# Operands moved to multiples of 512 bytes, and 768 tokens taken as 512 + 256 moving columns

## Chip, cores and metric

One core of a Trainium2 chip. The metric is the device time of one execution in microseconds, the median of the runs shown. The kernel is written in Bass with Tile: instructions go to TensorE, VectorE, ScalarE and GpSimd (PE, DVE, ACT and POOL below), DMAs are issued from SyncE's queue (SP). Outside the attention part the order on each engine is laid by the compiler's scheduler, starting from the program's order.

## What is computed

Two sequences (batch 2) of 768 tokens pass three layers, all in float32:

- block attention, 8 heads of width 64: each query sees the keys less than 16 positions away, and one summary (the largest of 32 keys, the mean of 32 values) for each block of 32 tokens; the result is x, 768 x 512;
- a gated layer: h = relu(x w_in), split into u and v (512 each); v is normalised over its 512 features and mixed over the tokens, v_s = w_spatial v_n + b; the result is (u * v_s) w_out;
- a convolution layer: h = relu(x w_in2) (1024 features), a depthwise convolution over the tokens with three taps, then (h * sigmoid(conv)) w_out2.

```
v_s = einsum('ts,bsd->btd', w_spatial, v_n) + b_spatial[None, :, None]
x   = (u * v_s) @ w_out
h   = relu(x @ w_in2);  c[t] = w0 * h[t-1] + w1 * h[t] + w2 * h[t+1]
out = (h * sigmoid(c)) @ w_out2
```

## The kernel before, in words

**Matmuls.** All large products are of float32 accuracy: each operand is held as a high part (rounded to float32r) and a low part (what is left), side by side in one tile of [128, 2, n], and `mm3` (line 58) issues three matmuls for each 128 x 128 stationary block: high x high (L62), high x low (L63), low x high (L64). The stationary operand is `lhsT`, 128 columns; the moving one, `rhs`, has as many columns as the output. `split` (line 66) makes high and low parts: a copy on ScalarE (L70), a subtraction on GpSimd or VectorE (L73).

**Stages**, in order:

- Attention, lines 179 to 325: 24 groups of 256 queries (8 pairs of heads and batch, 3 groups each), ordered by hand: `Plan` (line 133) lays a list by costs and due times, and the instructions are issued in this order. Idle TensorE time takes pieces of f1u for batch 0 (`f1u_plan`, line 413): one piece for each pair c, with its cost, with rank 1000 (after everything else that is ready), reading the token groups of x that its columns need. Six of the eight token halves go here.
- f1v(b), line 389: v = relu(x w_in) for a tile of 128 tokens; stationary x, moving w1, 512 columns (tile vps). Then statistics, normalising, high and low part of vn (L367 to L385).
- f1u(b), line 402: u = relu(x w_in) with features on the partitions; stationary w1, moving x, twice 384 tokens (ups; mm for the pieces in the attention part).
- spatial(b), line 429: stationary vn, moving wsp (the mixing matrix), twice 384 tokens, 6 blocks x 3 matmuls each (sps); then bias, product with u, high and low part of g1.
- merge_weights, line 457: w_out w_in2 as one matrix; stationary wo, moving wi, 512 columns (wps), result in wp.
- i2(b), line 476: eight tiles f of 128 features; stationary wp, moving g1, twice 384 tokens (hps), 4 blocks x 3 matmuls each. A relu on ScalarE writes h into hh, which has a zero column on either side (two memsets on VectorE, L480 and L481). The first tap is a scaled copy on ScalarE (L487), the two others are a multiply and add on VectorE (L489); then sigmoid (L490), product on GpSimd (L491), high and low part of y (low part on GpSimd in batch 0, on VectorE in batch 1).
- o2(b), line 505: stationary y, moving w2, 512 columns (ops); for three token tiles the feature tiles 0 to 6 first, then feature tile 7; the last token tile of batch 1 in two halves of 256 columns. A copy and a DMA out.

The order after attention (lines 606 to 620): f1v(0), f1u(0) (the rest), spatial(0), f1v(1), f1u(1), spatial(1), merge_weights, i2(0), o2(0), i2(1), o2(1), with the weights' loading and conversion beside them.

**Places in SBUF.** Tiles come from pools that lie one behind the other: const, slots (X tiles for x and g1, V tiles for u, vn and wp, W tiles for w1, wi and w2), tmp, then, when the attention pool is closed, late on its memory: b_bc, S tiles (wsp, then y 0 to 5), T tiles (wst, wo, hh and ct), raw and last, Y tiles (y 6 and 7). A tile's size is rounded up to 32 bytes in a partition. In tmp there are five tiles of 2048 bytes and ten small ones of 32.

Of the kernel before, what the change touches and what calls it, by code (L numbers as in the profile page):

```python
# [32 lines left out]
DM = 512  # L33
DF = 1024
NT = S // 128
HS = S // 2


@with_exitstack
def block_kernel(ctx, tc, q_in, k_in, vwin, v_in, mask, runs, w_in, w_spT, b_sp, w_outT, w_in2, conv, w_out2, out):  # L40
# [3 lines left out]
    const = ctx.enter_context(tc.tile_pool(name="const", bufs=1))  # L44
    slots = ctx.enter_context(tc.tile_pool(name="slots", bufs=1))
    tmp = ctx.enter_context(tc.tile_pool(name="tmp", bufs=5))
    psm = ctx.enter_context(tc.tile_pool(name="psm", bufs=2, space=PSUM))

    mm_pools = [psm, None, 0]
# [8 lines left out]
    def mm3(ps, pairs, first=True, last=True):  # L58

        n = len(pairs)  # L60
        for i, ((lh, ll), (rh, rl)) in enumerate(pairs):
            PE.matmul(ps, lhsT=lh, rhs=rh, start=first and i == 0, stop=False)  # L62
            PE.matmul(ps, lhsT=lh, rhs=rl, start=False, stop=False)  # L63
            PE.matmul(ps, lhsT=ll, rhs=rh, start=False, stop=last and i == n - 1)  # L64
# [328 lines left out]
            yield  # L393

    def f1u_mm(ps, b, f, h, c):
        fs, hs = slice(f * 128, (f + 1) * 128), slice(h * HS, (h + 1) * HS)
        mm3(ps[:, :HS], [((w1[c, 0][:, 0, fs], w1[c, 0][:, 1, fs]), (x[b, c][:, 0, hs], x[b, c][:, 1, hs]))], first=c == 0, last=c == NP - 1)

    def f1u_relu(ps, b, f, h):
        ACT.activation(out=u[b, f // 2][:, f % 2, h * HS:(h + 1) * HS], in_=ps[:, :HS], func=AF.Relu)  # L400

    def f1u(b, first=0):
        if not first:
# [9 lines left out]
    def f1u_plan(k, bank):  # L413

        f, h = divmod(k, 2)
        ps, m = mms[bank], ("mm", bank)
        for c in range(NP):
            xs = [("x", 0, c, g) + e for g in ((0, 1), (1, 2))[h] for e in ((), ("h",))]
            plan.add({"PE": (0.53, lambda c=c: f1u_mm(ps, 0, f, h, c))}, 1000 + k, xs + [("w1h", c, 0), ("w1l", c, 0)] + [m] * bool(c), [m])
        plan.add({"ACT": (0.49, lambda: f1u_relu(ps, 0, f, h))}, STEP * 12 + k, [m], [("u", k)])  # L420

    def load_wsp():
        for t in range(NT):
            wsp.append(late.tile([128, 2, S], F32R, tag="S", name=f"wsp_{t}", bufs=6))
            st = t_slot(f"wst_{t}", F32)[:, 0, :S]
            SP.dma_start(st, w_spT[t * 128:(t + 1) * 128, :])
            split(st, wsp[t][:, 0], wsp[t][:, 1], leng=POOL if t % 2 else DVE)

    def spatial(b):
        for f in range(4):  # L430
            g1[b, f] = x_slot(f"g_{b}_{f}")
            for h in range(2):
                ps = mmps(f"sps_{b}_{f}_{h}")
                fs, hs = slice(f * 128, (f + 1) * 128), slice(h * HS, (h + 1) * HS)
                mm3(ps[:, :HS], [((vn[b][2 * t][:, fs], vn[b][2 * t + 1][:, fs]), (wsp[t][:, 0, hs], wsp[t][:, 1, hs])) for t in range(NT)])
                tt = tmp.tile([128, HS], F32, tag="tmp", name=f"tt_{b}_{f}_{h}")
                DVE.tensor_tensor(out=tt, in0=ps[:, :HS], in1=b_bc[:, hs], op=ALU.add)
                DVE.tensor_tensor(out=tt, in0=tt, in1=u[b, f // 2][:, f % 2, hs], op=ALU.mult)
                split(tt, g1[b, f][:, 0, hs], g1[b, f][:, 1, hs], heng=ACT, leng=DVE)
                yield  # L440
# [35 lines left out]
    def i2(b):  # L476
        for f in range(8):
            tt = t_slot(f"hh_{b}_{f}", F32)
            hh, ct = tt[:, 0], tt[:, 1, :S]
            DVE.memset(hh[:, 0:1], 0.0)  # L480
            DVE.memset(hh[:, S + 1:S + 2], 0.0)  # L481
            for h in range(2):
                ps = mmps(f"hps_{b}_{f}_{h}")
                fs, hs = slice(f % 4 * 128, (f % 4 + 1) * 128), slice(h * HS, (h + 1) * HS)
                mm3(ps[:, :HS], [((wp(c, f // 4)[0][:, fs], wp(c, f // 4)[1][:, fs]), (g1[b, c][:, 0, hs], g1[b, c][:, 1, hs])) for c in range(4)])
                ACT.activation(out=hh[:, 1 + h * HS:1 + (h + 1) * HS], in_=ps[:, :HS], func=AF.Relu)
            ACT.activation(out=ct, in_=hh[:, 0:S], func=AF.Copy, scale=conv_t[:, 3 * f:3 * f + 1])  # L487
            for j in (1, 2):
                DVE.scalar_tensor_tensor(out=ct, in0=hh[:, j:j + S], scalar=conv_t[:, 3 * f + j:3 * f + j + 1], in1=ct, op0=ALU.mult, op1=ALU.add)  # L489
            ACT.activation(out=ct, in_=ct, func=AF.Sigmoid)  # L490
            POOL.tensor_tensor(out=ct, in0=hh[:, 1:S + 1], in1=ct, op=ALU.mult)  # L491
            if f < 6:
                y[b, f] = late.tile([128, 2, S], F32R, tag="S", name=f"y_{b}_{f}", bufs=6)
            else:
                y[b, f] = late.tile([128, 2, S], F32R, tag="Y", name=f"y_{b}_{f}", bufs=2)
            split(ct, y[b, f][:, 0], y[b, f][:, 1], heng=ACT, leng=DVE if b else POOL)
            yield

# [102 lines left out]
    raw_pool[0] = late  # L601

    def t_slot(name, dt):
        return late.tile([128, 2, S + 2], dt, tag="T", name=name, bufs=3)

    b_bc = late.tile([128, S], F32, name="b_bc", bufs=1)
    SP.dma_start(b_bc, b_sp.partition_broadcast(128))
# [71 lines left out]
```

## Time and profile before

| | |
|---|---|
| median of 3 runs | 360.98 us (360.39 to 361.37) |
| span of the profiled execution | 358.8 us; no other time is listed for it |
| TensorE busy | 345.1 us, 2487 matmuls |
| VectorE, ScalarE, GpSimd busy | 229.4, 183.4, 157.9 us |

The span goes from the first instruction to the last. Matmuls are pipelined: the duration shown of one (0.33 us at 384 columns) reaches into the next, so the pace is read from the distance of starts. A window's row gives its bounds, its length, then for each engine the busy time and the number of instructions that touch the window, and last the granted clock of TensorE, the DMA share and GB/s. A count can hold one or two matmuls that only reach over an edge; where the bounds are the first starts of two neighbouring stages, and only the stage's tile is asked for, it is the stage's own number.

### The profile page before, as it was taken

Reading aid. Unit: us, or ns where it says so; the run is one execution under the profiler, and the core shown is the slowest. Engines: PE = TensorE matmul, PEld = TensorE weight load, DVE = VectorE, ACT = ScalarE, POOL = GpSimd, SP = SyncE. Lnnn points to the kernel's source line nnn. Section 1 sums busy time; section 2 is a strip of 40 time slices with the busy share of each in tenths; the row PEclk is TensorE's granted clock in tenths of the full one; section 3 lists DMA queues with packets and bytes.
Section 4 is the critical chain, followed back from the end, with each engine's and each line's share of the span. In section 5 each row is a group of like instructions: output and inputs, shape, how many; then the busy total and the mean of one; then the engine's idle time right before and its main releaser. Section 6 shows DMA issues by size and latency. Waiting matters only on the chain.

```text
span 358.8 us, 6400 instructions
## 1 busy us (share of the span) xinstructions
PE 345.1 (96%) x2487; PEld 301.0 (84%) x2487; DVE 229.4 (64%) x390; ACT 183.4 (51%) x374; POOL 157.9 (44%) x159
## 2 busy tenths in 40 slices
PE   8998899999797999999999999999999999999996
PEld 4766677777586999899999888999888899998885
DVE  3889998884179799779298899457620025886000
ACT  2766778757264442355342464867531047874101
POOL 3789999765136142116133062587870003333000
PEclk9999999999899899999999999999999999999999
DMA  8877888320381232015232351000002020000202
GB/s 259 276 231 239 235 265 248 98 68 2 94 293 43 58 103 74 0 35 164 97 107 71 108 166 78 2 0 0 2 0 88 2 88 1 3 0 2 88 0 88
DMA packets 11118, 33.86 MB, mean 94 GB/s; under 512 B 1488, under 2 KB 1872, under 8 KB 11088
## 3 DMA queue, kind: packets, MB, share of 16 engines
q1 hardware_dynamic: 11088, 33.46, 29.8%
q8 instruction: 19, 0.31, 0.3%
q14 instruction: 11, 0.09, 0.1%
HBM read 30.31 MB, written 3.15 MB: 93 GB/s over the span
## 4 chain that ended last, share of the span: by engine, by line
PE 86%; DVE 4%; DMA 3%; POOL 2%; issue 2%; ACT 1%; SPq 0%; POOLq 0%; ACTq 0%; DVEq 0%
PE ops L63 6%; PE ops L62 6%; PE ops L64 6%; PE hps L62 6%; PE hps L63 6%; PE hps L64 6%; PE sps L64 5%; PE sps L62 5%; PE sps L63 5%; PE xp L310 3%; PE s L284 3%; PE pt L305 3%; PE mm L247 2%; PE vps L62 2%; PE wps L64 2%; PE wps L63 2%
## 5 line engine op out<-in xcount | busy, mean ns | idle before, releaser
L489 DVE SCALAR_TENSOR_TENSOR hh<-hh,conv_t 128x768 f32<-128x768 f32 x32 | 43.2, 1349 | 41.9 <-ACT hh L487 41.4
L491 POOL TENSOR_TENSOR hh<-hh 128x768 f32<-128x768 f32 x16 | 25.4, 1588 | 53.7 <-ACT hh L490 53.7
L63 PE MATMUL hps<-g,wp 128*128 128x384 f32 x128 | 42.8, 334 | 0.0
L64 PE MATMUL hps<-g,wp 128*128 128x384 f32 x128 | 42.8, 334 | 0.0
L62 PE MATMUL hps<-g,wp 128*128 128x384 f32 x128 | 42.8, 334 | 0.0
L62 PE MATMUL ops<-w,y 128*128 128x512 f32 (+1 forms) x104 | 39.0, 377 | 0.0
L63 PE MATMUL ops<-w,y 128*128 128x512 f32 (+1 forms) x104 | 38.9, 377 | 0.0
L64 PE MATMUL ops<-w,y 128*128 128x512 f32 (+1 forms) x104 | 37.8, 376 | 0.0
L62 PE MATMUL sps<-wsp,vn 128*128 128x384 f32 x96 | 32.9, 343 | 1.8 <-ACT vn L382 1.8
L64 PE MATMUL sps<-wsp,vn 128*128 128x384 f32 x96 | 32.7, 345 | 0.5 <-DVE vn L385 0.5
L63 PE MATMUL sps<-wsp,vn 128*128 128x384 f32 x96 | 32.9, 343 | 0.0
L301 POOL TENSOR_TENSOR e<-e,st 128x480 f32<-128x480 f32 x24 | 25.4, 1061 | 15.6 <-DVE st L298 5.3
L292 ACT ACTIVATE e<-s,st 128x120 f32<-128x120 f32 x96 | 26.8, 371 | 7.2 <-DVE st L288 7.1
L517 ACT COPY o<-ops 128x512 f32<-128x512 f32 (+1 forms) x13 | 6.8, 557 | 40.0 <-PE ops L64 39.5
L62 PEld LDWEIGHTS hps<-g,wp 128*128 128x128 f32 x128 | 24.0, 188 | 0.1
L63 PEld LDWEIGHTS hps<-g,wp 128*128 128x128 f32 x128 | 24.0, 188 | 0.1
L64 PEld LDWEIGHTS hps<-g,wp 128*128 128x128 f32 x128 | 24.0, 188 | 0.0
L64 PEld LDWEIGHTS ops<-w,y 128*128 128x128 f32 x104 | 19.5, 188 | 4.0
L62 PEld LDWEIGHTS ops<-w,y 128*128 128x128 f32 x104 | 19.5, 187 | 4.0
L63 PEld LDWEIGHTS ops<-w,y 128*128 128x128 f32 x104 | 19.5, 188 | 3.9
L73 POOL TENSOR_TENSOR wi<-wit_f,wi 128x512 fp32r<-128x512 f32 x8 | 12.8, 1604 | 20.4 <-ACT wi L70 20.4
L73 POOL TENSOR_TENSOR w<-w2t_f,w 128x512 fp32r<-128x512 f32 x8 | 11.9, 1519 | 20.5 <-ACT w L70 20.5
(121 smaller groups left out, 874.8 us busy)
## 6 DMA issues: line engine op xcount, KB each, us to landing
vw<-vwin SPq DMA_DIRECT2D x8, 576.0 KB, 5.5
raw<-w_in SPq DMA_DIRECT2D x8, 512.0 KB, 4.9
wit_raw<-w_in SPq DMA_DIRECT2D x8, 512.0 KB, 3.7
w2t_raw<-w_out SPq DMA_DIRECT2D x8, 512.0 KB, 3.7
kt<-k_in SPq DMA_DIRECT2D x8, 400.0 KB, 4.6
qt<-q_in SPq DMA_DIRECT2D x8, 384.0 KB, 3.6
out<-o SPq DMA_DIRECT2D x11, 256.0 KB, 2.0
wst<-w_spT SPq DMA_DIRECT2D x6, 384.0 KB, 4.9
```

What stands on the lines that cost most here:

```text
L62: PE.matmul(ps, lhsT=lh, rhs=rh, start=first and i == 0, stop=False)
L63: PE.matmul(ps, lhsT=lh, rhs=rl, start=False, stop=False)
L64: PE.matmul(ps, lhsT=ll, rhs=rh, start=False, stop=last and i == n - 1)
L73: leng.tensor_tensor(out=lo, in0=src, in1=hi.bitcast(F32), op=ALU.subtract)
L247: PE.matmul(ps, lhsT=runs_t[:, NZ - WK - 2 * blk:NZ - WK - 2 * blk + NK], rhs=vws[j][:WK, blk], start=blk == 0, stop=blk == NB - 1)
L284: PE.matmul(s[c * QB:(c + 1) * QB, h, a * NK:(a + 1) * NK], lhsT=qts[j][rows, blk * QB:(blk + 1) * QB], rhs=kws[j][rows, blk], start=False ...
L292: ACT.activation(out=e[:, u, :NK], in_=sv[:, u // 2, u % 2], func=AF.Exp, bias=st[:, 0, u:u + 1])
L301: POOL.tensor_tensor(out=e[:, :, :NK], in0=e[:, :, :NK], in1=st[:, 2].unsqueeze(2).to_broadcast([128, GB, NK]), op=ALU.mult)
L305: PE.transpose(pt[:, u], e[:, u, :NK], ident)
L310: PE.matmul(xp[h * D:(h + 1) * D, k * QB:(k + 1) * QB], lhsT=vws[j][:, g * GB + k, h * D:(h + 1) * D], rhs=pts[:, 2 * h + k // 2, k % 2 * ...
L489: DVE.scalar_tensor_tensor(out=ct, in0=hh[:, j:j + S], scalar=conv_t[:, 3 * f + j:3 * f + j + 1], in1=ct, op0=ALU.mult, op1=ALU.add)
L491: POOL.tensor_tensor(out=ct, in0=hh[:, 1:S + 1], in1=ct, op=ALU.mult)
```

## The change

`tmp` gets one more tile of 48 floats, which nothing uses. The halves of 384 tokens become `TS`, 512 and 256 tokens, in f1u (and its planned pieces, with new costs; the short one reads token group 2 alone), in spatial and in i2. T tiles lose two columns: hh has no zero columns any more, the middle tap is the scaled copy, and the two outer taps are added over 767 columns each. S tiles are eight instead of six, and y 6 and 7 come from them too; the Y tiles go.

```diff
--- before.py
+++ after.py
@@ -33,7 +33,7 @@
 DM = 512
 DF = 1024
 NT = S // 128
-HS = S // 2
+TS = [slice(0, 512), slice(512, S)]
 
 
 @with_exitstack
@@ -44,6 +44,7 @@
     const = ctx.enter_context(tc.tile_pool(name="const", bufs=1))
     slots = ctx.enter_context(tc.tile_pool(name="slots", bufs=1))
     tmp = ctx.enter_context(tc.tile_pool(name="tmp", bufs=5))
+    tmp.tile([128, 48], F32, tag="pad", name="pad", bufs=1)
     psm = ctx.enter_context(tc.tile_pool(name="psm", bufs=2, space=PSUM))
 
     mm_pools = [psm, None, 0]
@@ -393,11 +394,11 @@
             yield
 
     def f1u_mm(ps, b, f, h, c):
-        fs, hs = slice(f * 128, (f + 1) * 128), slice(h * HS, (h + 1) * HS)
-        mm3(ps[:, :HS], [((w1[c, 0][:, 0, fs], w1[c, 0][:, 1, fs]), (x[b, c][:, 0, hs], x[b, c][:, 1, hs]))], first=c == 0, last=c == NP - 1)
+        fs, hs = slice(f * 128, (f + 1) * 128), TS[h]
+        mm3(ps[:, :hs.stop - hs.start], [((w1[c, 0][:, 0, fs], w1[c, 0][:, 1, fs]), (x[b, c][:, 0, hs], x[b, c][:, 1, hs]))], first=c == 0, last=c == NP - 1)
 
     def f1u_relu(ps, b, f, h):
-        ACT.activation(out=u[b, f // 2][:, f % 2, h * HS:(h + 1) * HS], in_=ps[:, :HS], func=AF.Relu)
+        ACT.activation(out=u[b, f // 2][:, f % 2, TS[h]], in_=ps[:, :TS[h].stop - TS[h].start], func=AF.Relu)
 
     def f1u(b, first=0):
         if not first:
@@ -415,13 +416,13 @@
         f, h = divmod(k, 2)
         ps, m = mms[bank], ("mm", bank)
         for c in range(NP):
-            xs = [("x", 0, c, g) + e for g in ((0, 1), (1, 2))[h] for e in ((), ("h",))]
-            plan.add({"PE": (0.53, lambda c=c: f1u_mm(ps, 0, f, h, c))}, 1000 + k, xs + [("w1h", c, 0), ("w1l", c, 0)] + [m] * bool(c), [m])
-        plan.add({"ACT": (0.49, lambda: f1u_relu(ps, 0, f, h))}, STEP * 12 + k, [m], [("u", k)])
+            xs = [("x", 0, c, g) + e for g in ((0, 1), (2,))[h] for e in ((), ("h",))]
+            plan.add({"PE": ((0.69, 0.36)[h], lambda c=c: f1u_mm(ps, 0, f, h, c))}, 1000 + k, xs + [("w1h", c, 0), ("w1l", c, 0)] + [m] * bool(c), [m])
+        plan.add({"ACT": ((0.6, 0.38)[h], lambda: f1u_relu(ps, 0, f, h))}, STEP * 12 + k, [m], [("u", k)])
 
     def load_wsp():
         for t in range(NT):
-            wsp.append(late.tile([128, 2, S], F32R, tag="S", name=f"wsp_{t}", bufs=6))
+            wsp.append(late.tile([128, 2, S], F32R, tag="S", name=f"wsp_{t}", bufs=8))
             st = t_slot(f"wst_{t}", F32)[:, 0, :S]
             SP.dma_start(st, w_spT[t * 128:(t + 1) * 128, :])
             split(st, wsp[t][:, 0], wsp[t][:, 1], leng=POOL if t % 2 else DVE)
@@ -431,10 +432,11 @@
             g1[b, f] = x_slot(f"g_{b}_{f}")
             for h in range(2):
                 ps = mmps(f"sps_{b}_{f}_{h}")
-                fs, hs = slice(f * 128, (f + 1) * 128), slice(h * HS, (h + 1) * HS)
-                mm3(ps[:, :HS], [((vn[b][2 * t][:, fs], vn[b][2 * t + 1][:, fs]), (wsp[t][:, 0, hs], wsp[t][:, 1, hs])) for t in range(NT)])
-                tt = tmp.tile([128, HS], F32, tag="tmp", name=f"tt_{b}_{f}_{h}")
-                DVE.tensor_tensor(out=tt, in0=ps[:, :HS], in1=b_bc[:, hs], op=ALU.add)
+                fs, hs = slice(f * 128, (f + 1) * 128), TS[h]
+                n = hs.stop - hs.start
+                mm3(ps[:, :n], [((vn[b][2 * t][:, fs], vn[b][2 * t + 1][:, fs]), (wsp[t][:, 0, hs], wsp[t][:, 1, hs])) for t in range(NT)])
+                tt = tmp.tile([128, n], F32, tag="tmp", name=f"tt_{b}_{f}_{h}")
+                DVE.tensor_tensor(out=tt, in0=ps[:, :n], in1=b_bc[:, hs], op=ALU.add)
                 DVE.tensor_tensor(out=tt, in0=tt, in1=u[b, f // 2][:, f % 2, hs], op=ALU.mult)
                 split(tt, g1[b, f][:, 0, hs], g1[b, f][:, 1, hs], heng=ACT, leng=DVE)
                 yield
@@ -476,23 +478,19 @@
     def i2(b):
         for f in range(8):
             tt = t_slot(f"hh_{b}_{f}", F32)
-            hh, ct = tt[:, 0], tt[:, 1, :S]
-            DVE.memset(hh[:, 0:1], 0.0)
-            DVE.memset(hh[:, S + 1:S + 2], 0.0)
+            hh, ct = tt[:, 0], tt[:, 1]
             for h in range(2):
                 ps = mmps(f"hps_{b}_{f}_{h}")
-                fs, hs = slice(f % 4 * 128, (f % 4 + 1) * 128), slice(h * HS, (h + 1) * HS)
-                mm3(ps[:, :HS], [((wp(c, f // 4)[0][:, fs], wp(c, f // 4)[1][:, fs]), (g1[b, c][:, 0, hs], g1[b, c][:, 1, hs])) for c in range(4)])
-                ACT.activation(out=hh[:, 1 + h * HS:1 + (h + 1) * HS], in_=ps[:, :HS], func=AF.Relu)
-            ACT.activation(out=ct, in_=hh[:, 0:S], func=AF.Copy, scale=conv_t[:, 3 * f:3 * f + 1])
-            for j in (1, 2):
-                DVE.scalar_tensor_tensor(out=ct, in0=hh[:, j:j + S], scalar=conv_t[:, 3 * f + j:3 * f + j + 1], in1=ct, op0=ALU.mult, op1=ALU.add)
+                fs, hs = slice(f % 4 * 128, (f % 4 + 1) * 128), TS[h]
+                n = hs.stop - hs.start
+                mm3(ps[:, :n], [((wp(c, f // 4)[0][:, fs], wp(c, f // 4)[1][:, fs]), (g1[b, c][:, 0, hs], g1[b, c][:, 1, hs])) for c in range(4)])
+                ACT.activation(out=hh[:, hs], in_=ps[:, :n], func=AF.Relu)
+            ACT.activation(out=ct, in_=hh, func=AF.Copy, scale=conv_t[:, 3 * f + 1:3 * f + 2])
+            for j, to, of in ((0, slice(1, S), slice(0, S - 1)), (2, slice(0, S - 1), slice(1, S))):
+                DVE.scalar_tensor_tensor(out=ct[:, to], in0=hh[:, of], scalar=conv_t[:, 3 * f + j:3 * f + j + 1], in1=ct[:, to], op0=ALU.mult, op1=ALU.add)
             ACT.activation(out=ct, in_=ct, func=AF.Sigmoid)
-            POOL.tensor_tensor(out=ct, in0=hh[:, 1:S + 1], in1=ct, op=ALU.mult)
-            if f < 6:
-                y[b, f] = late.tile([128, 2, S], F32R, tag="S", name=f"y_{b}_{f}", bufs=6)
-            else:
-                y[b, f] = late.tile([128, 2, S], F32R, tag="Y", name=f"y_{b}_{f}", bufs=2)
+            POOL.tensor_tensor(out=ct, in0=hh, in1=ct, op=ALU.mult)
+            y[b, f] = late.tile([128, 2, S], F32R, tag="S", name=f"y_{b}_{f}", bufs=8)
             split(ct, y[b, f][:, 0], y[b, f][:, 1], heng=ACT, leng=DVE if b else POOL)
             yield
 
@@ -601,7 +599,7 @@
     raw_pool[0] = late
 
     def t_slot(name, dt):
-        return late.tile([128, 2, S + 2], dt, tag="T", name=name, bufs=3)
+        return late.tile([128, 2, S], dt, tag="T", name=name, bufs=3)
 
     b_bc = late.tile([128, S], F32, name="b_bc", bufs=1)
     SP.dma_start(b_bc, b_sp.partition_broadcast(128))
```

## Rows read from the trace of the kernel before

**Rows 1.** The page: busy time; busy tenths and granted clock in 40 slices.

```profile
PE 345.1 (96%) x2487; PEld 301.0 (84%) x2487; DVE 229.4 (64%) x390; ACT 183.4 (51%) x374; POOL 157.9 (44%) x159
...
PE   8998899999797999999999999999999999999996
...
PEclk9999999999899899999999999999999999999999
```

**Rows 2.** Windows by stage, one tile each: f1v(1), f1u(1), spatial(1), merge_weights, i2(0), o2(0).

```profile
141.23:157.57 16.34, 16.34 (x72) 13.34 (x72) 2.99 (x5) 1.00 0.00 0
...
157.57:174.23 16.66, 16.66 (x96) 16.50 (x95) 3.41 (x7) 1.00 0.41 128
...
174.23:199.19 24.96, 24.96 (x144) 24.80 (x144) 3.86 (x7) 1.00 0.28 85
...
199.19:221.42 22.23, 22.23 (x96) 17.84 (x96) 4.11 (x6) 3.74 (x7) 1.00 0.46 142
...
221.42:254.71 33.29, 33.29 (x192) 33.12 (x191) 6.85 (x14) 1.00 0.00 1
...
254.71:288.25 33.54, 33.54 (x144) 26.81 (x144) 2.65 (x5) 1.00 0.06 24
```

**Rows 3.** Timeline of TensorE, 256-column matmuls of o2(1): start, duration.

```profile
348.23 0.28 PE L63 MATMUL ops<-w,y 128*128 128x256 f32 x1
...
349.93 0.28 PE L63 MATMUL ops<-w,y 128*128 128x256 f32 x1
...
350.64 0.28 PE L63 MATMUL ops<-w,y 128*128 128x256 f32 x1
...
352.53 0.28 PE L64 MATMUL ops<-w,y 128*128 128x256 f32 x1
```

**Rows 4.** Windows with tile sps alone: spatial(0), its start, the stretch behind it.

```profile
111.89:141.23 29.34, 27.07 (x144) 26.24 (x144) 3.79 (x7) 0.94 0.25 72
111.89:115.90 4.01, 1.82 (x8) 1.15 (x8) 0.00 (x0) 1.00 0.00 0
115.90:119.70 3.80, 3.71 (x12) 3.72 (x13) 0.00 (x0) 0.55 0.00 0
```

**Rows 5.** Window over the end of attention: PE, PEld, DVE, ACT, POOL.

```profile
85.00:95.00 10.00, 7.53 (x78) 5.69 (x76) 3.23 (x8) 5.55 (x16) 4.60 (x6) 1.00 0.01 2
```

**Rows 6.** The convolution's tile hh: count, ns min/median/max, first and last start.

```profile
L486 ACT ACTIVATE hh<-hps x32: 468/492/498, 224.8 to 322.1; 128x384 f32<-128x384 f32 x32
L489 DVE SCALAR_TENSOR_TENSOR hh<-hh,conv_t x32: 1018/1052/2190, 227.3 to 326.6; 128x768 f32<-128x768 f32 x32
L480 DVE MEMSET hh<- x16: 59/59/59, 224.2 to 319.8; 128x1 f32 x16
...
L487 ACT ACTIVATE hh<-hh,conv_t x16: 921/927/942, 226.3 to 324.0; 128x768 f32<-128x768 f32 x16
L490 ACT ACTIVATE hh<-hh x16: 842/848/853, 229.8 to 327.7; 128x768 f32<-128x768 f32 x16
...
L70 ACT CAST y<-hh x16: 817/836/840, 232.4 to 330.2; 128x768 fp32r<-128x768 f32 x16
...
L73 DVE TENSOR_TENSOR y<-hh,y x8: 951/953/959, 300.5 to 331.0; 128x768 fp32r<-128x768 f32 x8
```

**Rows 7.** Timeline of GpSimd at the end of i2(0)'s products and low parts.

```profile
262.35 2.33 POOL L73 TENSOR_TENSOR y<-hh,y 128x768 fp32r<-128x768 f32 x1 [0.95 <-ACT y L70]
264.64 1.54 POOL L491 TENSOR_TENSOR hh<-hh 128x768 f32<-128x768 f32 x1
267.13 1.55 POOL L73 TENSOR_TENSOR y<-hh,y 128x768 fp32r<-128x768 f32 x1 [0.94 <-ACT y L70]
```

**Rows 8.** Timeline of TensorE at the start of spatial(0), with its waits.

```profile
113.37 0.44 PE L64 MATMUL sps<-wsp,vn 128*128 128x384 f32 x1 [0.45 <-DVE vn L385]
...
115.98 0.45 PE L62 MATMUL sps<-wsp,vn 128*128 128x384 f32 x1 [1.82 <-ACT vn L382]
```

## Prediction, made before the result

> **What bounds the kernel now.** I read the page first: TensorE is busy for 96% of the span, in nearly every slice, and its granted clock is full in all but a few [rows 1]. So time can only be won where TensorE's own work gets shorter, or where the few holes are. A busy share says nothing of pace, since the matmuls overlap. So the second view is one window for each stage, cut from the stage's first matmul to the next stage's first: length divided by count is the **spacing**, the distance from one matmul's start to the next [rows 2]. Spacings of that view, and of single rows of the timeline:
>
> - 384 columns: 33.29/192 = 173.4 ns in i2 (batch 0), 173.3 in spatial(1), 173.5 in f1u(1) [rows 2].
> - 512 columns: 16.34/72 = 226.9 in f1v(1), but 22.23/96 = 231.6 in merge_weights and 33.54/144 = 232.9 in o2(0) [rows 2]. Same shape and type, full clock in all three.
> - 256 columns, the last token tile of o2(1): 15 steps from 348.23 to 349.93, 113.4 ns, for the first output half; 16 steps from 350.64 to 352.53, 118.1 ns, for the second [rows 3].
>
> At 2.4 GHz the columns alone take 160.0, 213.3 and 106.7 ns. What is on top is 13.4 at 384, 13.6 at 512 in f1v, 18 to 20 at 512 in merge_weights and o2, and 6.7 or 11.4 at 256. Two things follow. Something other than the shape parts f1v from o2; and a 256 seems cheaper than its share of a 384.
>
> The something is, I think, the place of the stationary operand. The pools lie one behind the other, so a tile's place follows from the sizes before it. The pool `slots` (X, V, W) starts on a multiple of 512 bytes and its tiles are multiples of 512. `tmp` is 5 x 2048 + 10 x 32 = 10,560 bytes, 320 more than a multiple, so the pool `late` starts 320 past one: wsp and y 0 to 5 lie at 320, y 6 and 7 at 416, the T tiles of wo at 320, 352 and 384 (S + 2 makes each a little over 6144). So f1v has both operands on 512; merge_weights has wo off it; o2 has y off it. In spatial(1) only the moving operand (wsp) is off, and its spacing equals that of i2, where nothing is off. So a moving operand off 512 costs nothing visible at 384 columns, and a stationary one costs 5 to 6 ns at 512.
>
> **The change, part by part.**
>
> *Pad and T tiles without the two extra columns.* 48 floats are 192 bytes: 320 + 192 = 512, so wsp, wo and y come onto 512. No instruction is added. o2: 11 whole token tiles x 24 = 264 matmuls x (232.9 - 226.9) = 1.58 us. merge_weights: 96 x (231.6 - 226.9) = 0.45 us. The 48 of 256 columns in o2: the first half already stands at 113.4, so I take 0 (at most 24 x 4.7 ns = 0.11).
>
> *384 + 384 becomes 512 + 256.* The number of matmuls and columns stays. A pair takes 2 x 173.4 = 346.8 ns now. After, both operands are on 512, so the 512 is nearest to f1v's row, 226.9. For the 256 no row has everything aligned: from below 106.7 ns, the columns' time alone, from above 120.3, if it carried 13.6 like its neighbours; I take the measured 113.4. Pair: 340.3, a gain of 6.5 ns; the ends of the 256 make it +13.2 and -0.4, and the slowest rows (232.9 + 118.1 = 351.0) make it a loss of 4.2. Pairs on the path: i2 2 x 192, spatial(1) 144 and f1u(1) 96 matmuls, and what spatial(0) still has to do after its wait (144 less the 8 and 12 of the first 7.8 us, 124) [rows 2, 4], give 192 + 72 + 48 + 62 = 374 pairs. 374 x 6.5 = 2.43 us. The 36 pairs in the attention part and the 12 of f1u(0) before that wait I count at nothing: in 85 to 95 us TensorE is busy only 7.53 of 10 us [rows 5], waiting for the softmax chain. If that cover were gone they would be worth 48 x 6.5 = 0.3 us. The planner's pieces change from 0.52 us each to 0.68 and 0.34; a longer one can hold up a waiting transpose by 0.16 us, a shorter one lets it go 0.18 earlier; over 12 of each about +-2 us at the most, taken as 0.
>
> **A rule to weigh.** By the rows, spacing is no function of columns alone. The Trainium skill (TensorE: Matmul & The Clock Gate, section Back-to-back issue gap) gives N/2.4 + 2.5 ns for the isolated gap, addresses not mentioned; by it 512 + 256 and twice 384 are both 325 ns and the whole change would be worth 0. The rows disagree with it in size (13.4 ns, not 2.5, at 384) and in form (226.9 and 232.9 at one N).
>
> *The convolution.* 32 memsets of 59 ns go from VectorE, the first tap moves to the middle, the two scalar_tensor_tensor run over 767 instead of 768 columns. Per channel tile i2 costs ScalarE 2 x 0.49 + 0.93 + 0.85 + 0.84 = 3.6 us and VectorE 2 x 1.05 (medians) + 0.12, plus 0.95 in batch 1 [rows 6], against 24 x 173.4 = 4.16 us of TensorE (24/2 x 340.3 = 4.08 after). Both are hidden by the matmuls; without that cover the memsets would be 1.9 us in all. The relus and evictions split 512/256 handle the same 768 columns.
>
> *What is late next.* In i2(0) the low part of y is on GpSimd, and its cadence is the product, a wait of 0.95 us for ScalarE's copy, and the low part of 2.33 us [rows 7], 4.8 us per tile against TensorE's 4.16. The last low part ends at 267.13 + 1.55 = 268.68 us [rows 7], 47.26 us after i2(0)'s first matmul at 221.42. o2(0) needs it, in program order, after 192 matmuls of i2 and 63 of its own: now 33.29 + 63 x 0.2329 = 47.96, so no wait; after, 96 x 0.3403 + 63 x 0.2269 = 46.96, 0.3 us too early, and y 6 stands behind the same cadence. I charge 0.4 us, between 0 and 1.0 (the whole advance of TensorE up to there). In batch 1 the low part is on VectorE and o2(1) has over 3 us in hand (last one at 331.0 [rows 6], first needed after 321.55 + 63 x 0.2329 = 336.2).
>
> *Buffers.* Eight S slots instead of six and two Y hold the same bytes; wsp uses six either way, y 0 to 7 follow in the same order.
>
> **Sum.** 1.58 + 0.45 + 2.43 - 0.4 = 4.1 us off a span of 358.8. The profiled execution has no other time than its span; the median of the runs, 360.98, lies 2.2 us above it, which I take to be around the span and unchanged. Forecast 360.98 - 4.1 = **356.9 us**.
>
> **Rivals.**
>
> *A fixed cost per matmul.* A matmul with aligned operands carries 13.5 ns whatever its width (384 and 512 both do). For it: two widths agree. Against it: 256 carried 6.7. Then pairs give 0 and the alignment 2.03: 358.9 us.
>
> *The address is not what parts f1v from o2*, and it is which tiles meet. o2 and merge_weights stay, the pairs alone give 2.43, less a little wait: 358.7 us. Against it: three places of wo and y, three slower spacings.
>
> *The other side: slower.* Same premise, but the new 512 and 256 pace like o2's: pair 351.0, loss 374 x 4.2 = 1.6 us, nothing gained elsewhere: 362.6 us. It decides from a pair sum above 346.8. For it: these are the only rows in which a 512 and a 256 stand side by side. Against it: i2, spatial and f1u read their stationary operands from `slots`, as f1v does.
>
> *The start of spatial(0) moves.* Its 144 matmuls take 29.34 us against 24.96 in batch 1 [rows 2, 4]: TensorE waits 0.45 and 1.82 us for vn [rows 8], and then does 12 matmuls in 3.80 us at half the clock (1.2 GHz; mean 0.55 with the edges) [rows 4]. The order there is laid by the compiler's scheduler, which sees new sizes. Were all 4.4 us to go, 352.5; were they to grow by as much, 361.3.
>
> *Nothing comes of it.* Only columns count, or a new wait eats it: 361.0. The Trainium skill's SBUF page (SBUF — State Buffer, Operand start alignment) asks only for element alignment and says that this is about legality, not speed; no run here times its case.
>
> **Numbers.** About 0.3%, 1.1 us, is what a measurement of this kernel can tell from no change. Forecast as worked out, 354.0 (a 256 at 106.7, no wait in o2) to 359.3 (a 256 at 118.1, a wait of 1.0) by its own bounds: 0.56. Fixed cost: 0.12. Pairs alone: 0.07. Spatial(0) better: 0.08. These are faster, 0.83. Nothing, or eaten by a new wait: 0.11, the same. Slower pairs: 0.06. The range takes in all of the faster ones, 352.5 to 359.6 us, and leaves out 0.17.
>
> **What would show it.** Spacings after, by the same windows: o2 and merge_weights near 227; 512s in i2, spatial, f1u near 227 and their 256s near 113, so that an i2 stage takes 32.7 us instead of 33.3; a 256 at 120 means the fixed cost, o2 still at 233 means that the address is not it. A hole of TensorE in o2(0) before the matmuls with y 6 or 7 would be GpSimd's cadence. The start of spatial(0) should again cost about 4.4 us over spatial(1). I am wrong if the time is above 359.6, or if it is right while these spacings are not.

## The result, and the profile after

The changed kernel takes **363.37 us** (median of 21 runs, 362.55 to 369.49). The kernel before, run beside it 21 times, takes 360.98 us. The ratio is 1.0071 [1.0052, 1.0089]: **slower by 2.4 us**, where 4.1 us less were forecast. The profiled execution took 364.12 us with a span of 362.3 us. Ratios, here and below, leave out runs more than 1.5% above the fastest of their kernel, so they differ a little from the quotient of the medians.

The page, with busy time, then the busy tenths and the granted clock in 40 slices, answers to [rows 1]:

```profile
PE 344.4 (95%) x2487; PEld 284.8 (79%) x2487; DVE 234.8 (65%) x358; ACT 182.7 (50%) x374; POOL 163.7 (45%) x159
...
PE   7998899999796999999999999999799999999995
...
PEclk9999999999998799999999999999989999999999
```

TensorE has lost a little busy time. GpSimd has gained 5.8 us with the same 159 instructions. In slices 29 and 30 of 40 there is a new dip, of TensorE and then of its clock.

The windows by stage, cut as in [rows 2] (PE, PEld, and where they work DVE and ACT; then granted clock, DMA share, GB/s): f1v(1), f1u(1), spatial(1), merge_weights, i2(0), o2(0), and the whole token tiles of o2(1):

```profile
142.37:158.72 16.35, 16.35 (x72) 13.34 (x72) 2.99 (x5) 1.00 0.00 0
...
158.72:175.41 16.69, 16.69 (x96) 14.70 (x95) 3.54 (x7) 1.00 0.42 128
...
175.41:200.45 25.04, 25.04 (x144) 22.10 (x144) 3.98 (x7) 1.00 0.27 85
...
200.45:222.24 21.79, 21.79 (x96) 17.84 (x96) 4.11 (x6) 3.72 (x7) 1.00 0.50 145
...
222.24:255.65 33.41, 33.41 (x192) 29.46 (x191) 6.50 (x14) 1.00 0.00 1
...
255.65:292.14 36.49, 34.60 (x144) 27.94 (x144) 2.64 (x5) 0.95 0.06 22
325.55:351.42 25.87, 25.87 (x115) 21.40 (x116) 1.76 (x3) 1.00 0.08 31
```

- merge_weights paces 21.79/96 = 227.0 ns instead of 231.6, and o2(1) 25.87/114 = 226.9 (114 matmuls start in that window): the alignment works.
- i2(0) takes 33.41 us and not 32.7. In one spatial(1) or i2 stage twice 384 and 512 + 256 differ by 0.1 us, and the new cut is the longer one.
- o2(0) takes 36.49 us, 2.95 more than before. That is the loss.

TensorE in o2(0), its 13th matmul and some behind it (start, duration, tile, and in brackets the wait and who ended it):

```profile
260.44 0.50 PE L63 MATMUL ops<-w,y 128*128 128x512 f32 x1 [1.89 <-ACT y L71]
...
262.25 0.63 PE L64 MATMUL ops<-w,y 128*128 128x512 f32 x1
262.67 0.63 PE L65 MATMUL ops<-w,y 128*128 128x512 f32 x1
...
265.83 0.39 PE L65 MATMUL ops<-w,y 128*128 128x512 f32 x1
```

The 13th matmul is the first to read y 4. It waits 1.89 us for ScalarE's copy, and soon after the matmuls start 0.42 us apart. A window of this stretch (length, busy, clock) shows a granted clock of 0.50, the 1.2 GHz level:

```profile
261.60:265.00 3.40, 3.40 (x10) 0.50 0.00 0
```

3.40 us at half speed cost 1.70. Wait and half clock make 3.59 us of the 36.49 - 144 x 0.2269 = 3.82 us that o2(0) is over its pace.

Why ScalarE is late is seen on GpSimd. First the convolution's tile (count, ns min/median/max, first and last start), beside [rows 6]; then GpSimd's timeline at the end of i2(0), beside [rows 7]:

```profile
L490 DVE SCALAR_TENSOR_TENSOR hh<-hh,conv_t x32: 1017/1430/2579, 228.0 to 332.7; 128x767 f32<-128x767 f32 x32
...
L492 POOL TENSOR_TENSOR hh<-hh x16: 1805/1847/2555, 233.0 to 334.8; 128x768 f32<-128x768 f32 x16
...
L74 POOL TENSOR_TENSOR y<-hh,y x8: 1842/2628/2634, 235.8 to 273.9; 128x768 fp32r<-128x768 f32 x8
```

```profile
265.69 1.86 POOL L492 TENSOR_TENSOR hh<-hh 128x768 f32<-128x768 f32 x1
268.50 2.63 POOL L74 TENSOR_TENSOR y<-hh,y 128x768 fp32r<-128x768 f32 x1 [0.95 <-ACT y L71]
271.09 1.83 POOL L492 TENSOR_TENSOR hh<-hh 128x768 f32<-128x768 f32 x1
273.87 1.84 POOL L74 TENSOR_TENSOR y<-hh,y 128x768 fp32r<-128x768 f32 x1 [0.94 <-ACT y L71]
```

The same product over the same 128 x 768 numbers takes 1.85 us where it took 1.54, and the low part 2.63 where it took 2.33 [rows 7] (the last one, alone, 1.84 instead of 1.55). A tile's cadence on GpSimd goes from 4.8 to 5.4 us (268.50 to 273.87), while TensorE still makes one in 33.41/8 = 4.18. The chain falls behind until o2(0) meets it: the last low part ends at 275.71, 53.5 us after i2(0)'s first matmul, where it was 47.3. ScalarE's timeline in the middle of it:

```profile
254.61 0.87 ACT L487 ACTIVATE hh<-hps 128x512 f32<-128x512 f32 x2 [0.86 <-POOL y L74]
258.00 0.84 ACT L491 ACTIVATE hh<-hh 128x768 f32<-128x768 f32 x1 [2.52 <-DVE hh L490]
...
259.57 0.81 ACT L71 CAST y<-hh 128x768 fp32r<-128x768 f32 x1
```

A relu waits for a T tile that GpSimd's low part still holds, the next tile's sigmoid waits for VectorE's taps, and behind it in ScalarE's queue stands the copy of y 4 that TensorE waits for. The taps are longer too, 1.43 us in the median against 1.05 in [rows 6] and 1.13 in the first experiment below; the small kernel shows that GpSimd's places lengthen VectorE's work.

**A yardstick.** Up to the end of spatial(0) executions of one and the same kernel differ by several us, by stretches of half clock after waits (in two profiles of one kernel of the experiments that point came at 140.84 and 146.78; it came at 141.23 before, 142.37 after). From there to the last matmul the time hardly varies: two kernels were profiled twice, on different chips, and agreed within 0.03 us (213.03 and 213.03; 212.86 and 212.89). This **tail** is 358.71 - 142.37 = 216.34 us after and 355.28 - 141.23 = 214.05 before. The difference, 2.29, is nearly the whole 2.4 us of the result, and the stages add up to it: merge_weights -0.44, o2(1) -0.57, o2(0) +2.95, both i2 +0.24, spatial(1) and f1u(1) +0.11.

### The profile page after: what moved, and what is told of

Its sections match the earlier page's. It is cut to its first block, busy times and chain, and to the rows that moved or that the text cites. A ratio compares the mean times of both kernels' runs of the same rounds, so it can differ in the third digit from the quotient of the medians.

```text
span 362.3 us, 6391 instructions
## 1 busy us (share of the span) xinstructions
PE 344.4 (95%) x2487; PEld 284.8 (79%) x2487; DVE 234.8 (65%) x358; ACT 182.7 (50%) x374; POOL 163.7 (45%) x159
## 4 chain that ended last, share of the span: by engine, by line
PE 76%; DVE 8%; DMA 7%; ACT 4%; issue 2%; SPq 1%; POOL 1%; ACTq 0%; DVEq 0%; POOLq 0%
PE ops L63 6%; PE ops L65 6%; PE ops L64 6%; DVE hh L490 6%; DMA vw<-vwin 5%; PE sps L63 5%; PE sps L64 5%; PE sps L65 5%; PE hps L64 3%; PE hps L63 3%; PE hps L65 3%; PE xp L311 3%; PE mm L248 3%; PE pt L306 3%; PE s L285 3%
## 5 line engine op out<-in xcount | busy, mean ns | idle before, releaser
L490 DVE SCALAR_TENSOR_TENSOR hh<-hh,conv_t 128x767 f32<-128x767 f32 x32 | 49.7, 1554 | 53.1 <-ACT hh L488 52.5
L492 POOL TENSOR_TENSOR hh<-hh 128x768 f32<-128x768 f32 x16 | 30.2, 1888 | 52.2 <-ACT hh L491 52.2
L64 PE MATMUL hps<-g,wp 128*128 128x512 f32 (+1 forms) x128 | 43.2, 337 | 0.0
L63 PE MATMUL hps<-g,wp 128*128 128x512 f32 (+1 forms) x128 | 43.1, 337 | 0.0
L65 PE MATMUL hps<-g,wp 128*128 128x512 f32 (+1 forms) x128 | 43.0, 336 | 0.0
L63 PE MATMUL ops<-w,y 128*128 128x512 f32 (+1 forms) x104 | 39.7, 381 | 1.9 <-ACT y L71 1.9
L64 PE MATMUL ops<-w,y 128*128 128x512 f32 (+1 forms) x104 | 39.2, 378 | 0.0
L65 PE MATMUL ops<-w,y 128*128 128x512 f32 (+1 forms) x104 | 38.2, 380 | 0.0
L63 PE MATMUL sps<-wsp,vn 128*128 128x256 f32 (+1 forms) x96 | 33.7, 353 | 2.1 <-ACT vn L383 2.0
L65 PE MATMUL sps<-wsp,vn 128*128 128x512 f32 (+1 forms) x96 | 32.9, 346 | 1.4 <-DVE vn L386 1.4
L64 PE MATMUL sps<-wsp,vn 128*128 128x512 f32 (+1 forms) x96 | 33.2, 348 | 0.0
L63 PEld LDWEIGHTS hps<-g,wp 128*128 128x128 f32 x128 | 24.3, 190 | 2.8
L64 PEld LDWEIGHTS hps<-g,wp 128*128 128x128 f32 x128 | 24.3, 190 | 2.6
L65 PEld LDWEIGHTS hps<-g,wp 128*128 128x128 f32 x128 | 24.2, 189 | 2.6
L63 PEld LDWEIGHTS ops<-w,y 128*128 128x128 f32 x104 | 20.0, 193 | 5.9 <-ACT y L71 2.3
L65 PEld LDWEIGHTS ops<-w,y 128*128 128x128 f32 x104 | 20.0, 193 | 3.7
L63 PEld LDWEIGHTS sps<-wsp,vn 128*128 128x128 f32 x96 | 19.2, 201 | 4.7 <-ACT vn L383 2.7
L74 POOL TENSOR_TENSOR y<-hh,y 128x768 fp32r<-128x768 f32 x8 | 20.0, 2510 | 5.7 <-ACT y L71 5.7
L64 PEld LDWEIGHTS ops<-w,y 128*128 128x128 f32 x104 | 19.9, 191 | 3.4
```

The lines of the kernel that those rows point to most:

```text
L74: leng.tensor_tensor(out=lo, in0=src, in1=hi.bitcast(F32), op=ALU.subtract)
L490: DVE.scalar_tensor_tensor(out=ct[:, to], in0=hh[:, of], scalar=conv_t[:, 3 * f + j:3 * f + j + 1], in1=ct[:, to], op0=ALU.mult, op1=ALU.add)
L492: POOL.tensor_tensor(out=ct, in0=hh, in1=ct, op=ALU.mult)
```

## The experiments

**Is it where GpSimd's operands lie?** The change took two columns off each half of the T tiles, so the convolution's result ct now lies 3,072 bytes behind hh (3,080 before, with the product reading hh from its second number). The first experiment puts the columns back and changes nothing else; the second keeps the new places and undoes the cut into 512 and 256.

```diff
-            hh, ct = tt[:, 0], tt[:, 1]
+            hh, ct = tt[:, 0, :S], tt[:, 1, :S]
...
-        return late.tile([128, 2, S], dt, tag="T", name=name, bufs=3)
+        return late.tile([128, 2, S + 2], dt, tag="T", name=name, bufs=3)
```

> The changed kernel with the T tiles two columns wider again and ct in columns S + 2 onward, so that ct lies 3080 and not 3072 bytes behind hh; the order on every engine is that of the changed kernel. Theory P (place: two float32 inputs of a GpSimd operation that lie a multiple of 512 bytes apart make it slower): GpSimd's product back from 1.85 to 1.54 us, the low part of y in batch 0 from 2.63 (1.84 alone) to 2.3 (1.55 alone), cadence 5.4 to 4.8 us per feature tile, no wait of 1.89 us in o2(0), o2(0) about 33 us instead of 36.5, time about 360. Rival H (the halves of 512 and 256 delay the chain) and rival C (the middle tap first, the outer ones shifted by one element, slow VectorE and through it GpSimd): product stays at 1.85, o2(0) at 36.5, time about 363.

```diff
-TS = [slice(0, 512), slice(512, S)]
+TS = [slice(0, S // 2), slice(S // 2, S)]
...
-            xs = [("x", 0, c, g) + e for g in ((0, 1), (2,))[h] for e in ((), ("h",))]
+            xs = [("x", 0, c, g) + e for g in ((0, 1), (1, 2))[h] for e in ((), ("h",))]
```

(The planner's costs go back to 0.53 and 0.49 as well.)

> The changed kernel with the tokens taken as twice 384 again (planner costs and token groups too), all places as in the change. P: GpSimd's product stays at 1.85 us and o2(0) keeps its wait, 36 us or more; a pair of 384 paces at 2 x 173.3 = 346.7 ns against 348.4 as 512 + 256, so i2 goes from 33.41 to 33.3; time within 0.3% of the changed kernel unless the start of spatial(0) moves. H: o2(0) back to about 33 us and the time to 360. C: as P.

The first: 359.46 us (12 runs), ratio 0.9942 [0.9911, 0.9974]; every engine has its instructions in the same order as in the changed kernel. Its window of o2(0), and then the two GpSimd groups of the convolution's tile:

```profile
254.06:286.73 32.67, 32.67 (x144) 26.85 (x144) 2.63 (x5) 1.00 0.07 25
```

```profile
L492 POOL TENSOR_TENSOR hh<-hh x16: 1537/1548/2266, 231.1 to 327.7; 128x768 f32<-128x768 f32 x16
...
L74 POOL TENSOR_TENSOR y<-hh,y x8: 1548/2290/2337, 233.6 to 268.6; 128x768 fp32r<-128x768 f32 x8
```

Eight bytes per tile half bring GpSimd back to 1.55 and 2.3 us, and o2(0) to 32.67/144 = 226.9 ns without a hole. The tail is 213.03 us, 3.3 less than the changed kernel's, although merge_weights is back at 22.28: with the two columns wo's three tiles lie at 0, 32 and 64 bytes past a multiple of 512, two of them off again. The taps of this kernel are those of the change, the middle one first and the outer two over 767 columns, so these aren't the cause either.

The second: 363.56 us (12 runs), ratio 1.0064 [1.0028, 1.01]. In its trace, TensorE at the same matmul of o2(0), and the product's group:

```profile
262.96 0.50 PE L63 MATMUL ops<-w,y 128*128 128x512 f32 x1 [2.15 <-ACT y L71]
```

```profile
L492 POOL TENSOR_TENSOR hh<-hh x16: 1807/1848/2566, 235.5 to 337.3; 128x768 f32<-128x768 f32 x16
```

The slow product, the wait and the lost time are there without any 512 + 256. The cut into 512 and 256 isn't the cause.

**The pad alone, in the kernel before.** One line is added:

```diff
+    tmp.tile([128, 48], F32, tag="pad", name="pad", bufs=1)
```

> The kernel before with the 48-float tile alone: wsp and y 0 to 5 come onto 512, T tiles lie at 0, 32 and 64, y 6 and 7 at 96; ct stays 3080 bytes behind hh, twice 384 stays. P: GpSimd's product stays 1.54 us; 512-column matmuls of o2 with y 0 to 5 at 227 instead of 233 ns; o2(1) about 0.5 us shorter, o2(0) too unless it waits for y; time 0.8 to 1.5 us below the kernel before. H and C: the same, since neither halves nor taps are touched. If the time is not below the kernel before, the gain from the alignment is lost again in a wait, and the trace must show where.

361.2 us (12 runs), ratio 0.9991 [0.9952, 1.003]: no gain that the total shows. The product stays at 1.545 us, o2(0) takes 33.02 instead of 33.54 and o2(1) 33.39 instead of 33.73, merge_weights stays (22.27), and the tail is 0.8 us shorter, with no wait of TensorE in i2(0) and o2(0). Two of wo's three tiles, y 6 and y 7 are still off, by the T tiles' two columns; why merge_weights gains nothing by the tile that is now on 512 isn't shown. Of the 0.8 to 1.5 us that were expected the tail shows 0.8; in the total that is less than the variation ahead of the tail.

**The places by themselves.** A small kernel on operands put at chosen places; from it come the prices of TensorE's and GpSimd's places.

> A kernel of its own that computes none of the reference: 18 matmuls each at 512, 384 and 256 columns, for seven pairs of places (stationary, moving; bytes past a multiple of 512); then GpSimd products of two float32 tiles of 768 columns, three each with the second input 0, 4, 8, 16, 32, 64, 128 and 256 bytes past the place of the first; then the multiply-add on VectorE, two each, over 767 columns at the same distances; then six GpSimd products beside eight VectorE multiply-adds, at distance 0 and again at 8. P: products at 0 bytes take 1.85 us and at 4 or 8 bytes 1.54; where in between it changes is open. H and C: all products alike. Matmuls: a stationary operand on 512 gives 226.7, 173.3 and 120.0 ns; off it 233 at 512 and 113 at 256 if place alone decides.

TensorE, one window for each group of 18 matmuls (length, busy, clock). With 512 columns, (stationary, moving) bytes past a multiple of 512: (0, 0), (320, 0), (0, 320), (320, 320):

```profile
24.95:29.03 4.08, 4.08 (x18) 1.00 0.00 0
29.03:33.23 4.20, 4.20 (x19) 1.00 0.00 0
33.23:37.37 4.14, 4.14 (x20) 1.00 0.02 4
37.37:41.45 4.08, 4.08 (x20) 1.00 0.00 0
```

and with 256 columns the same four, then (64, 0):

```profile
75.82:77.97 2.15, 2.15 (x19) 1.00 0.00 0
77.97:80.09 2.12, 2.12 (x20) 1.00 0.00 0
80.09:82.22 2.13, 2.13 (x21) 1.00 0.04 8
82.22:84.37 2.15, 2.15 (x21) 1.00 0.00 0
84.37:86.43 2.06, 2.06 (x21) 1.00 0.00 0
```

Divided by 18: 226.7, 233.3, 230.0, 226.7 at 512 columns; 119.4, 117.8, 118.3, 119.4 and 114.4 at 256. Two things differ from what I had read out of the rows of before. Both operands 320 bytes off are as quick as none off, so at 320 bytes what counts is where the two lie **relative to each other**. And at 256 columns the order is the reverse: like places are the slowest.

GpSimd, six products with a second input 0 bytes behind a multiple of 512 and then 8 (the first input on one), beside VectorE; between them one alone, at distance 0:

```profile
65.36 15.16 POOL L76 TENSOR_TENSOR gb<-ga,gb 128x768 f32<-128x768 f32 x6
83.54 1.84 POOL L80 TENSOR_TENSOR gc<-gc,va 128x768 f32<-128x768 f32 x1 [3.01 <-DVE va L79]
85.33 13.36 POOL L76 TENSOR_TENSOR gb<-ga,gb 128x768 f32<-128x768 f32 x6
```

8 bytes are worth (15.16 - 13.36)/6 = 0.30 us for each product, as in the kernel (0.31). Distances of 16, 32 and 64 bytes are like 0, 2.41 to 2.47 us beside VectorE, and 128 and 256, which had no VectorE work beside them, take 1.84 to 1.85, as 0 does alone; 4 and 8 take 2.14 beside VectorE. VectorE's eight multiply-adds beside the two sixes, with their own operands at the same places both times:

```profile
63.52 18.88 DVE L78 SCALAR_TENSOR_TENSOR vb<-va,one,vb 128x767 f32<-128x767 f32 x8
...
83.50 17.07 DVE L78 SCALAR_TENSOR_TENSOR vb<-va,one,vb 128x767 f32<-128x767 f32 x8
```

They lose (18.88 - 17.07)/6 = 0.30 us for each slow product too: GpSimd's places lengthen VectorE's work beside it.

**The cut with GpSimd quick.** The first experiment's kernel with twice 384 instead of 512 + 256 (the two diffs above together):

> The run with ct 3080 bytes behind hh, and the tokens as twice 384 besides. P: o2(0) has no wait either; the cut alone is what differs, by spacings of the runs so far 2 x 173.3 against 227 to 229 + 119 to 120: i2 33.3 instead of 33.4 us, spatial(1) 24.96 instead of 25.04, some 0.4 us in all the way to the end; the planned pieces and the start of spatial(0) can move by 1 us either way. Time 358.5 to 360.5, within 0.3% of the run with 512 and 256. If the cut were worth what the prediction said (6.5 ns a pair), this would be 2.4 us slower, 361.9.

360.75 us (12 runs), ratio 1.0004 [0.9978, 1.0031]. The tail is 212.86 us, 0.17 less than with 512 + 256, but the total was not better: 1.3 us above that of the first experiment, more than the 0.3% that was expected.

**Better places for the other low parts too.** On top of the first experiment, the converted weights and the staging of wsp move by two numbers, so that GpSimd's low parts there also lie 8 bytes apart:

```diff
-    tmp.tile([128, 48], F32, tag="pad", name="pad", bufs=1)
+    tmp.tile([128, 8], F32, tag="pad", name="pad", bufs=1)
...
-        f = f if f is not None else tmp.tile([p, n], F32, tag="tmp", name=f"{name}_f")
+        f = f if f is not None else tmp.tile([p, n + 2], F32, tag="tmp", name=f"{name}_f")[:, 2:]
...
-            st = t_slot(f"wst_{t}", F32)[:, 0, :S]
+            st = t_slot(f"wst_{t}", F32)[:, 0, 2:S + 2]
```

> The run with ct 3080 bytes behind hh, and the float32 sources of the other high and low splits (wst, and the converted weights in tmp) 8 bytes past their place as well; order on every engine unchanged. P: GpSimd's low parts of wsp go from 1.85 to 1.54 us and those of the weights (512 columns, in tmp) from about 1.28 alone to 1.05; the start of spatial(0) gets 0 to 0.6 us earlier, as its normalising on VectorE waits behind these; the rest is hidden. Time 358.5 to 359.5. Rivals H and C: GpSimd unchanged, time as before, 359.5.

358.88 us (8 runs), ratio 0.9948 [0.993, 0.9966], below both kernels. In the changed kernel the low part of wsp took 1.84 us, here (ns min/median/max):

```profile
L74 POOL TENSOR_TENSOR wsp<-wst,wsp x3: 1546/1552/2668, 102.5 to 111.8; 128x768 fp32r<-128x768 f32 x3
```

The tail (213.04) is that of the first experiment, so what this adds lies ahead of the tail, where executions differ. That it beats the first experiment is not shown.

**Low parts of y on VectorE**, with the slow places left as they are:

```diff
-            split(ct, y[b, f][:, 0], y[b, f][:, 1], heng=ACT, leng=DVE if b else POOL)
+            split(ct, y[b, f][:, 0], y[b, f][:, 1], heng=ACT, leng=DVE)
```

> The changed kernel with the low part of y in batch 0 on VectorE instead of GpSimd, places as in the change. P, by way of the cadence: GpSimd does the product alone, 1.85 us a tile, VectorE about 1.0 us more a tile; y 7 is there before o2(0) needs it, no wait, o2(0) 32.7 us, time 359 to 360.5. If the wait in o2(0) came from the chain through VectorE or ScalarE (H, C), it would stay or grow: o2(0) 36 us or more.

360.24 us (10 runs), ratio 0.9989 [0.9953, 1.0024]. GpSimd's products still take 1.85 us, but with the low parts gone it keeps up: o2(0) has one wait of 0.39 us, where none was expected, and no half clock; it takes 33.71 us, not the 36.49 of the changed kernel. Its window and that wait:

```profile
256.06:289.77 33.71, 33.29 (x144) 26.67 (x144) 2.83 (x5) 1.00 0.07 24
```

```profile
266.74 0.73 PE L65 MATMUL ops<-w,y 128*128 128x512 f32 x2 [0.39 <-DVE y L74]
```

**The slow place in the kernel before.** T tiles of S + 4 columns and ct from its second number, so that the product's inputs lie a multiple of 16 bytes apart; the order on the engines is as before, but for a few of VectorE's 59 ns memsets that stand one tap later in the trace:

```diff
-            hh, ct = tt[:, 0], tt[:, 1, :S]
+            hh, ct = tt[:, 0], tt[:, 1, 1:S + 1]
...
-        return late.tile([128, 2, S + 2], dt, tag="T", name=name, bufs=3)
+        return late.tile([128, 2, S + 4], dt, tag="T", name=name, bufs=3)
```

> The kernel before with ct moved by one float, so that hh from column 1 and ct lie a multiple of 16 bytes apart; order on every engine that of the kernel before. P: the product goes from 1.54 to 1.85 us, the low part stays at 2.3; the cadence from 4.8 to 5.1 us, y 7 comes 2.4 us later, about 49.7 us after i2(0)'s first matmul, where TensorE now needs it at about 48.7: a wait of about 1 us in o2(0), more if the clock falls after it; time 361.5 to 364. H and C: nothing changes, time as before.

367.11 us (4 runs, 362.41 to 369.49), ratio 1.0133 [1.0073, 1.0193]. The product's group, and a low part on GpSimd's timeline:

```profile
L491 POOL TENSOR_TENSOR hh<-hh x16: 1837/1845/2559, 237.7 to 339.3; 128x768 f32<-128x768 f32 x16
```

```profile
273.16 2.62 POOL L73 TENSOR_TENSOR y<-hh,y 128x768 fp32r<-128x768 f32 x1 [0.94 <-ACT y L70]
```

The place alone makes the kernel before slower: o2(0) takes 35.49 us instead of 33.54, and the tail grows by the same 1.95, without a stretch of half clock in o2(0). The rest of the 6 us lies ahead of the tail, where its trace has 20 us of half clock against 6.8 before; that the place brought those on isn't shown. Two misses: the low part was to stay quick and took 2.62 us, and the total was to be 361.5 to 364 us; of its four runs one is in that range.

**What is the cut worth?** The kernel of the first experiment and that with halves had differed by 1.3 us in the total while their tails stood the other way. One theory was that the cut pays in f1u, where the planner lays the order, ahead of the tail. So one kernel has 512 + 256 in f1u alone (the second diff line stands in spatial and, alike, in i2), one everywhere but in f1u, and both older kernels run again.

```diff
+HT = [slice(0, S // 2), slice(S // 2, S)]
...
-                fs, hs = slice(f * 128, (f + 1) * 128), TS[h]
+                fs, hs = slice(f * 128, (f + 1) * 128), HT[h]
```

> ct 3080 bytes behind hh; 512 and 256 in f1u and its planned pieces alone, spatial and i2 as twice 384. Theory F (what the cut is worth lies in the attention part and f1u(0), by the order in which pieces fill TensorE, and not in the pace of pairs): as the run with 512 and 256 everywhere, 359.5, its attention end and start of spatial(0) the same to 0.5 us; from the end of spatial(0) to the last matmul 212.9 us. Rival G (the cut is worth nothing anywhere, and the two runs with fast places differ by chance): all four of this call within 0.3% of each other.

> ct 3080 bytes behind hh; 512 and 256 in spatial and i2 alone, f1u as twice 384. F: as the run with twice 384 everywhere, 360.7; from the end of spatial(0) to the last matmul 213.0 us. G: within 0.3% of the other three.

> The run with ct 3080 bytes behind hh and 512 and 256 everywhere once more, beside the other three on one chip. F: 359.5 and 0.3% or more below the run with twice 384. G: within 0.3% of it.

> The run with ct 3080 bytes behind hh and twice 384 everywhere once more. F: 360.7. G: within 0.3% of the run with 512 and 256.

| 512 + 256 in | us, median of 12 | ratio | tail |
|---|---|---|---|
| f1u alone | 360.61 | 0.9998 [0.9971, 1.0025] | 212.96 |
| all but f1u | 359.78 | 0.9955 [0.9927, 0.9984] | 213.02 |
| all, again | 359.87 | 0.9995 [0.9963, 1.0026] | 213.03 |
| none, again | 359.82 | 0.9965 [0.9933, 0.9996] | 212.89 |

The theory falls: with the cut in f1u alone nothing is won, and the difference between all and none did not come back. The four lie within 0.3% of each other, as the rival had it. The tails put the worth of the cut from f1v(1) on at 0.14 to 0.17 us, as a loss; ahead of that no worth is shown.

## Why the prediction was wrong

**Alignment: right in size.** Forecast 1.58 us for o2 and 0.45 for merge_weights. Where nothing holds TensorE up, o2(0) went from 33.54 to 32.67 and o2(1) from 33.73 to 33.16, together 1.44; merge_weights gave 0.44. Its reading was too narrow: by the small kernel a stationary operand off 512 is slow only against a moving one that lies elsewhere, and at 256 columns like places are the slow ones. o2(1)'s own 256s, taken at no change, went from 113 and 118 to 120 ns once y lay on 512.

**The pairs: mis-sized, 2.43 us forecast, about -0.35 found in the tail's 312 pairs.** The mis-sized term rests on "For the 256 no row has everything aligned" and then "I take the measured 113.4". That row belongs to a matmul whose y lay off 512, and a 256 is quicker so. With like places a 256 takes 119.4 ns and not 113.4, close to the upper bound of 120.3 that I had set. A pair is 226.7 + 119.4 = 346.1 against 346.8; in the kernel i2's pairs come out at 33.41/96 = 348.0, and where the other 1.9 ns come from is open. So the rival of a fixed cost per matmul describes this part: 13.4 ns on top of the columns at 512 (226.7 - 213.3), 13.4 at 384 (173.4 - 160.0) and 12.7 at 256 (119.4 - 106.7). The Trainium skill (TensorE: Matmul & The Clock Gate, section Back-to-back issue gap) has the form right for like places, a constant on N/2.4; its constant of 2.5 ns, given for an isolated matmul, is not what these streams of float32r matmuls show.

**What is late next: the step that decided the sign.** This is the step that failed: "I charge 0.4 us, between 0 and 1.0". I named GpSimd's cadence as what o2(0) would meet. The 1.0 assumed the cadence of [rows 7], 4.8 us, while the change moved every operand of both GpSimd instructions in it. I had looked at what places do to TensorE only. The trace of before had the other half: there GpSimd's low part of wsp, with both inputs at multiples of 32 bytes, takes 1.85 us, and the same subtraction over as many numbers for y, whose distance is 8 more than a multiple of 16, takes 1.55 [rows 7].

```profile
L73 POOL TENSOR_TENSOR wsp<-wst,wsp x3: 1846/1861/2271, 101.9 to 112.7; 128x768 fp32r<-128x768 f32 x3
```

The cadence came out at 5.4 us. It met o2(0) earlier than I said, at y 4 and not y 6 or 7, through ScalarE's queue. By the first experiment o2(0) pays 36.49 - 32.67 = 3.8 us for the place, of which 1.7 is the half clock behind the wait; I had not priced that either.

**The start of spatial(0)** was to cost about 4.4 us over spatial(1) again. It cost 31.66 - 25.04 = 6.6, with waits of 1.39 and 2.02 us and 6.8 us of half clock:

```profile
112.83 0.50 PE L65 MATMUL sps<-wsp,vn 128*128 128x512 f32 x1 [1.39 <-DVE vn L386]
...
116.05 0.80 PE L63 MATMUL sps<-wsp,vn 128*128 128x512 f32 x1 [2.02 <-ACT vn L383]
```

```profile
115.90:122.10 6.20, 6.05 (x21) 5.29 (x22) 0.00 (x0) 0.54 0.02 5
```

In the first experiment, with the same order and the same two waits, it was 30.43 and 3.4 us. This stage moves by several us from one execution to the next: it took 27.6 to 31.9 us in six profiles with 512 + 256 in f1u and 27.2 to 30.8 in seven with twice 384, and ended at 139.9 to 144.9 and at 140.1 to 148.2 us. A share of the change in it isn't shown.

**Buffers, memsets, relus** cost nothing that the tail shows.

**The sum as it was:** -1.0 for merge_weights and o2(1), +0.35 for the pairs, +2.95 in o2(0), where 0.87 was won and 3.8 lost: +2.3 us.

## What to carry to other kernels

A change of a tile's size or padding moves every tile behind it: list all engines whose operands move, and for GpSimd's two-input float32 work look at the distance between the two inputs before and after. An engine that paces a chain with a few tenths of a microsecond in hand needs its durations bounded from both sides in a forecast, not carried over. And measure a small change in the part of the trace that repeats from run to run; here the total hid 0.8 us that the tail showed.

## What the runs showed of the hardware

- **GpSimd's product depends on the places of its inputs.** Place of the first less place of the second, modulo 16 bytes: 0 gives 1.85 us for 128 x 768 float32 (the changed kernel, the one with the slow place, the small kernel), 8 gives 1.55 (the first experiment), and 12 gives 1.54 (the product before). 4 was slow (the low part with the slow place, 2.62 beside VectorE). The low part goes the same way: 1.84 at 0 and 1.55 at 8. That it goes by 16 bytes is read from these cases and the small kernel's; other distances weren't tried. In all of them the output lies at the second input's place modulo 16, so whether it is the two inputs or the first input and the output that matter isn't shown. VectorE's scalar_tensor_tensor over the same tiles takes 1.02 us at its shortest, with the places of before, after and the slow place alike.
- **VectorE and GpSimd lengthen one another:** the tap takes 1.02 us alone and up to 2.58 beside GpSimd, the low part 1.84 alone and 2.63 beside VectorE. The Trainium skill (SBUF — State Buffer, section SBUF: two separate sides) says that GpSimd and a VectorE instruction with two inputs in SBUF lock each other out of a port pair for whole instructions. The direction agrees; 2.63 is less than 1.84 + 1.02.
- **A wait can cost twice.** After waits of 1.89 us in o2(0), and with those of 1.39 and 2.02 us in spatial(0), TensorE's clock was at half for 3.4 and 6.8 us. With three short holes in o2(0) of the kernel before with the slow place (0.39 us at most) and one of 0.39 with the low parts on VectorE it stayed full.
